# Weight loads of a recurrent attention loop: issued on a plan of TensorE's progress

## The chip, the cores and the metric

The kernel runs on one core of a Trainium2 chip. The metric is device microseconds per execution. All weights, the input and the output are bf16. Five engines work side by side and meet only through semaphores: TensorE (PE, with its weight loads as PEld), VectorE (DVE), ScalarE (ACT), GpSimd (POOL) and SyncE (SP). In this kernel SyncE issues nearly all DMA transfers of the loop, one after the other in the order of the program.

## What is computed

The input `x` has 2048 tokens of 640 numbers. Branch A is an attention layer with 32 heads of 192 that runs over 64 segments of 32 tokens. Each segment sees its own tokens and 8 memory tokens, and the layer's output for the memory tokens is the memory of the next segment, so the 64 segments follow one another. Branch B is a gated GELU layer. A sigmoid gate mixes the two.

```python
def _A_ref(x, mem0, Wq, Wk, Wv, Wo, seg_len):
    ...
    for s in range(n_seg):
        xs = x[:, s * seg_len:(s + 1) * seg_len, :].copy()
        h = jnp.concatenate([mem, xs], axis=1)
        q = jnp.einsum('btd,dhe->bhte', h, Wq)      # the same for k and v
        scores = jnp.einsum('bhqe,bhke->bhqk', q, k) * scale
        scores = jnp.where(mask[None, None], scores, -1000000000.0)
        p = _softmax(scores, axis=-1)
        o = jnp.einsum('bhqk,bhke->bhqe', p, v)
        o = jnp.einsum('bhte,hed->btd', o, Wo)
        mem = o[:, :M, :].copy()
        outs.append(o[:, M:, :])
...
g = _sigmoid((x * gate_w).sum(-1, keepdims=True))
return g * a + (1 - g) * b
```

## The kernel before, in words

A recording layer (`_Sched`) notes every operation with the regions of memory that it reads and writes, works out which operations must wait for which, and then writes one stream of instructions per engine, in the order in which the operations were noted. An engine that waits therefore holds up all that stands behind it in its stream.

Branch B and the gate run first. Then comes the loop: `segment(s)` walks through a list `PROG` of some hundred items, written out by hand, that says in which order the parts of a segment go to TensorE. The heads are cut into four octets. `("g", i, k)` is a step of the projections to Q, K and V (`proj`, row L1039, and L226 where the weights stay on TensorE); `sc` are the scores (L1080, L1088, L1093), `ex` the softmax, `pt` transposes the probabilities, `pv` multiplies them with V (L1172, L1174), `wo` is the output projection (L1201, and L1224 for the last octet). The items `lf`, `le`, `vb` and the rows L882, L887, L889, L893 are work for later segments, on eight tokens of each (the "left" tokens), which doesn't hang on the memory; they differ between segments, with a period of four, so segments fall into classes by s mod 4. `out_store`, `x_load`, `stg_load` (L932), `bz_load` and `left_store` (L893) are the other transfers of the loop, all on SyncE.

The weights take more room than the on-chip memory has. They are cut into pieces: 384 KB for one k step of Q, K or V of one octet, 480 KB for a pair of heads of Wo. Most pieces stay on the chip for good. 17 slots are shared by two pieces each: one of the octet that even segments use first and odd segments use last, and one of the octet at the other end. So in every segment the first octet's pieces in these slots are overwritten, once used, by the pieces that the last octet of the same segment needs: four of Q, five of K, five of V, three of Wo. The next segment walks through the octets the other way round, and finds what the last one loaded.

`swap_loads(seg, item)` is called after each item of `PROG`. It goes through the pieces used since the last call (`done_keys`) and notes a load (`load_piece`, L597) of the other piece of each shared slot at once. The load waits for the last matmuls that read the slot; nothing else holds it but its place in SyncE's stream. The K pieces of the first four projection steps are put behind the Q pieces (`later`).

Of the kernel before, what the change touches and what calls it, by code (L numbers as in the profile page):

```python
# [231 lines left out]
def _build(nc, A_x, A_mem0, A_Wq, A_Wk, A_Wv, A_Wo, seg_len, w_gate, w_up, w_down,  # L232
# [34 lines left out]
    S_ = _Sched(nc)  # L267
# [84 lines left out]
    def bview(o, nbytes, plo=0, phi=128):  # L352
        return arena[plo:phi, o // 2:(o + nbytes) // 2]
# [4 lines left out]
    def sreg(o, nbytes, plo=0, phi=128):  # L358
        return Rg("sb", o, o + nbytes, plo, phi)
# [129 lines left out]
    def piece_src(key):  # L489
        if key[0] == 3:  # L490
            return Wo2[:, key[1]]
        m, o_, k = key
        return (Wq2, Wk2, Wv2)[m][:, k, OW * o_:OW * (o_ + 1)]

    def piece_size(key):
        return GO if key[0] == 3 else GQ

    def piece_view(key, o):
        if key[0] == 3:
            return bview(o, GO).rearrange("p (c n) -> p c n", n=Dm)  # L500
        return bview(o, GQ)
# [59 lines left out]
    res_off = {}  # L561
# [8 lines left out]
    r_res = {key: sreg(o, piece_size(key)) for key, o in res_off.items()}  # L570
# [21 lines left out]

    loaded = {}

    def load_piece(key, name):
        loaded[slot_id[key]] = key
        S_.add("sp", lambda e: e.dma_start(piece_view(key, res_off[key]), piece_src(key)), writes=[r_res[key]],  # L597
               dma_sem="slot%d" % slot_id[key], name="%s %s" % (name, key))

    def piece(seg, key):  # L600
        order = orders[seg % 2]
        oi = last_req.get(seg, -1) + 1
        assert order[oi] == key, "pieces must be consumed in order"
        last_req[seg] = oi
        if seg == 0 and key in tmp_off:
            return left_piece(key)
        done_keys.append(key)
        return piece_view(key, res_off[key]), r_res[key]

    def swap_loads(seg, item):  # L610
        if item[0] == "g" and item[1] == 0 and 0 < item[2] < KT - 1:
            later.extend(key for key in done_keys if key[0] == 1)
            done_keys[:] = [key for key in done_keys if key[0] != 1]
        elif later:
            done_keys[:] = sorted(done_keys + later, key=lambda key: key[:1] + key[2:])
            del later[:]
        for key in done_keys:
            other = swap_in.get(key)
            if other is None or (other in partner) == (seg % 2 == 0):
                continue  # L620
            load_piece(other, "swap s%d" % seg)
        del done_keys[:]

    def left_piece(key):
        if key in tmp_off:
            return piece_view(key, tmp_off[key]), r_tmp[key]
        return piece_view(key, res_off[key]), r_res[key]
# [6 lines left out]
    def load_residents(cls, pick=lambda key: True):  # L634
        for key in first:
            if slot_class[key] == cls and pick(key):
                load_piece(partner[key] if key in tmp_off else key, "res")
# [39 lines left out]
    for h in range(NH):  # L677
        for w_, sb_, rw_, nm in ((w_gate, wg_sb, r_wg, "wg"), (w_up, wu_sb, r_wu, "wu")):
            S_.add("sp", lambda e, h=h, w_=w_, sb_=sb_: e.dma_start(
                sb_[h], w_.rearrange("(p k) f -> p k f", p=128)[:, :, FH * h:FH * (h + 1)]),  # L680
                writes=[rw_[h]], dma_sem="%s%d" % (nm, h))
# [228 lines left out]
    for n, (g, o) in enumerate(units):  # L910
# [7 lines left out]
        if g == 0:  # L918
            S_.add("pool", lambda e, o=o, b=b: e.tensor_copy(out=stg[:, o], in_=lst[b][:, 0]), reads=[r_lst[b]], writes=[r_stg[o]],
                   name="stg s0 o%d" % o)  # L920
# [344 lines left out]
    def segment(s):  # L1265
# [3 lines left out]
        for n, item in enumerate(PROG):  # L1269
# [48 lines left out]
            else:  # L1318
# [3 lines left out]
                if q == 3 and item != items[-1]:  # L1322
                    wo_left(s, held)
            swap_loads(s, item)
            if s == 0 and item == ("g", 0, KT - 1):
                load_residents(3, lambda key: key[0] < 3 and on_tmp(key))
# [63 lines left out]
def bass_gated_mix__memory_aug_recurrent_mem_tr__glu_gated_geglu__prompt_kernel(  # L1390
    nc,
    A_x,
    A_mem0,
    A_Wq,
    A_Wk,
    A_Wv,
    A_Wo,
    A_seg_len,
    B_x,
    B_w_gate,  # L1400
    B_w_up,
    B_w_down,
    gate_w,
    out,
):
    _build(nc, A_x, A_mem0, A_Wq, A_Wk, A_Wv, A_Wo, A_seg_len, B_w_gate, B_w_up, B_w_down, gate_w, out)
# [33 lines left out]
```

## Time and profile before

| | |
|---|---|
| median of three runs | 1797.18 us (1792.85 to 1797.43) |
| span of the profiled execution, first to last instruction | 1783.4 us |
| median less that span | 13.8 us |
| granted TensorE clock, mean | 0.998 |
| HBM read over the span | 498.00 MB |
| transfers issued at L597: K, V, Q, Wo | 335, 335, 272, 205 |
| L597 from issue to landing, least / median / most | 3.0 / 7.7 / 15.7 us |

The page tells the profiled execution's span but not its time by the clock that the runs are timed with. What lies around the span is therefore taken as the difference to the median, 13.8 us (9.5 us to the fastest run). In the profile, a line such as `PE ps L1224 <- DMA arena<-in_A_Wo_dram: 12.6, 22, 0.9` says that TensorE's instructions of line 1224 stood idle for 12.6 us in all, 22 times and 0.9 us at the longest, until a transfer from Wo had landed. In a timeline a line shows the start, the length, engine, line and operation, how many were merged, and in brackets the idle time before it with what ended it.

### The profile page before, as it was taken

What the parts mean: (1) busy time and instruction counts of PE and PEld (TensorE: products, weight loads), DVE (VectorE), ACT (ScalarE), POOL (GpSimd) and SP (SyncE); (2) the same over time, 40 slices, a digit from 0 to 9 for tenths busy, and PEclk for the clock granted to TensorE, in tenths of its full rate; (3) what the DMA queues carried; (4) which work ended last, traced back from release to release, by engine and by line L of the source; (5) the groups of instructions that cost most, each with busy time, mean ns of one, the idle gap of its engine ahead of it and who ended that gap; (6) DMA issues with size and microseconds to landing.
All of it is one profiled execution on the core that took longest, in us unless ns stands there. A gap on an engine that the chain in (4) does not pass through costs nothing.

```text
span 1783.4 us, 80070 instructions
## 1 busy us (share of the span) xinstructions
PE 1629.5 (91%) x39162; PEld 817.9 (46%) x31501; DVE 957.7 (54%) x2932; ACT 793.8 (45%) x1835; POOL 319.8 (18%) x1099
## 2 busy tenths in 40 slices
PE   9999989899998999899899999899999989899987
PEld 4554444454444444454444444454444444454443
DVE  2223555555555655555565655555555655555554
ACT  3222444444444444444444444444444544444443
POOL 1100111111211111111111111111211111111211
PEclk9999999999999999999999999999999999999999
DMA  9815887888788887888788887888888887888786
GB/s 332 297 45 177 329 318 266 324 322 316 289 295 298 318 311 261 318 318 315 287 299 299 311 319 263 322 310 319 298 299 300 317 290 269 321 313 321 289 303 260
DMA packets 263390, 524.33 MB, mean 294 GB/s; under 512 B 97384, under 2 KB 116224, under 8 KB 263040
## 3 DMA queue, kind: packets, MB, share of 16 engines
q1 hardware_dynamic: 259912, 516.11, 79.5%
q8 instruction: 276, 4.52, 1.0%
q10 hardware_dynamic: 3128, 3.09, 0.5%
q14 instruction: 74, 0.61, 0.1%
HBM read 498.00 MB, written 21.11 MB: 291 GB/s over the span
## 4 chain that ended last, share of the span: by engine, by line
PE 69%; DMA 13%; DVE 8%; ACT 6%; issue 4%; SPq 0%; DVEq 0%; ACTq 0%
PE ps L1039 20%; PE ps L226 15%; PE ps L1201 8%; DMA arena<-in_A_Wv_dram 7%; PE ps L1172 3%; DMA left_qk_scratch<-arena 3%; PE ps L802 3%; PE ps L799 3%; PE ps L882 3%; DVE arena L889 3%; PE ps L1093 2%; PE ps L817 2%; ACT arena L887 2%; PE ps L1080 2%; PE ps L1088 2%
## 5 line engine op out<-in xcount | busy, mean ns | idle before, releaser
L1039 PE MATMUL ps<-arena 128*32 128x384 bf16 x9940 | 734.8, 328 | 58.5 <-DVE arena L1344 40.4
L226 PE MATMUL ps<-arena 128*32 128x384 bf16 x7680 | 584.4, 326 | 10.8 <-ACT arena L887 6.1
L1039 PEld LDWEIGHTS ps<-arena 128*32 128x32 bf16 x9940 | 254.0, 96 | 420.1 <-issue 244.4
L1073 DVE STREAM_TRANSPOSE arena<-arena 128x384 bf16<-128x384 bf16 x512 | 279.0, 564 | 227.0 <-ACT arena L1059 226.6
L1059 ACT ACTIVATE arena<-ps 128x384 bf16<-128x384 f32 x512 | 236.2, 489 | 176.3 <-PE ps L1039 164.4
L1201 PE MATMUL ps<-arena 128*32 128x320 bf16 x6144 | 297.0, 300 | 16.1 <-issue 15.5
L1201 PEld LDWEIGHTS ps<-arena 128*32 128x32 bf16 x6144 | 163.6, 97 | 75.7 <-issue 26.5
L1119 ACT ACTIVATE ps<-ps 104x160 f32<-104x160 f32 x256 | 74.3, 290 | 236.4 <-DVE ps L1109 236.4
L1107 DVE TENSOR_REDUCE arena<-ps 104x4 f32<-104x160 f32 x256 | 83.1, 325 | 176.0 <-PE ps L1093 175.7
L1157 ACT ACTIVATE arena<-ps 128x448 bf16<-128x448 f32 x192 | 104.8, 546 | 143.3 <-PE ps L1144 143.3
L1191 POOL COPY arena<-arena 128x96 bf16<-128x96 bf16 x256 | 68.4, 267 | 522.6 <-ACT arena L1183 419.3
L936 POOL COPY arena<-arena 128x96 bf16<-128x96 bf16 x256 | 70.0, 274 | 498.7 <-PE ps L1093 436.3
L1183 ACT ACTIVATE arena<-ps 128x480 bf16<-128x480 f32 (+1 forms) x256 | 138.1, 540 | 34.0 <-PE ps L1174 29.0
L1062 ACT ACTIVATE arena<-ps 128x384 bf16<-128x384 f32 x256 | 124.8, 488 | 52.7 <-PE ps L1039 52.4
L1172 PE MATMUL ps<-arena 128*64 128x160 bf16 x1536 | 122.1, 243 | 10.4 <-issue 3.4
L1172 PEld LDWEIGHTS ps<-arena 128*64 128x64 bf16 x1536 | 80.6, 109 | 97.9 <-ACT arena L1157 46.6
L882 PE MATMUL ps<-arena 128*32 128x384 bf16 x1280 | 111.1, 330 | 1.2 <-issue 1.2
L1174 PE MATMUL ps<-arena 128*64 128x64 bf16 x1536 | 105.1, 194 | 5.8 <-issue 5.8
L1121 DVE TENSOR_REDUCE arena<-ps 104x4 f32<-104x160 f32 x256 | 81.8, 320 | 51.6 <-ACT ps L1119 43.9
L889 DVE STREAM_TRANSPOSE arena<-arena 128x384 bf16<-128x384 bf16 x128 | 73.8, 577 | 57.4 <-ACT arena L887 52.6
L1224 PE MATMUL ps<-arena 128*32 128x160 bf16 x3072 | 77.1, 234 | 22.2 <-DMA arena<-in_A_Wo_dram 12.6
L887 ACT ACTIVATE arena<-ps 128x384 bf16<-128x384 f32 x128 | 62.4, 490 | 67.6 <-DVE arena L889 38.5
(84 smaller groups left out, 1816.7 us busy)
## 6 DMA issues: line engine op xcount, KB each, us to landing
arena<-in_A_Wk_dram SPq DMA_DIRECT2D x335, 384.0 KB, 7.7
arena<-in_A_Wv_dram SPq DMA_DIRECT2D x335, 384.0 KB, 9.4
arena<-in_A_Wq_dram SPq DMA_DIRECT2D x272, 384.0 KB, 5.6
arena<-in_A_Wo_dram SPq DMA_DIRECT2D x205, 480.0 KB, 7.4
left_qk_scratch<-arena SPq DMA_DIRECT2D x64, 192.0 KB, 2.6
arena<-left_qk_scratch SPq DMA_DIRECT2D x63, 192.0 KB, 7.8
ffn_b_scratch<-arena ACTq DMA_DIRECT2D x16, 160.0 KB, 3.7
arena<-ffn_b_scratch SPq DMA_DIRECT2D x64, 40.0 KB
```

The lines of the kernel that those rows point to most:

```text
L226: return e.add_instruction(mybir.InstMatmult(name=nm, start_tensor_calc=like["start"], stop_tensor_calc=stop, tile_size=(128, 32), tile_po ...
L882: fns.append(lambda e, outp=outp, rhs=rhs, j=j: e.matmul(outp, lhs, rhs, start=(k == 0), stop=(k == KT - 1), tile_position=(0, 32 * j)))
L889: S_.add("dve", lambda e: e.transpose(out=dst[:, :, m].rearrange("p q c i -> p c q i"), in_=rowl.rearrange("p (c r) -> p c r", r=L)), read ...
L1039: fns.append(lambda e, outp=outp, rhs=rhs, j=j: e.matmul(outp, lhs, rhs, start=(k == 0), stop=(k == KT - 1), tile_position=(0, 32 * j)))
L1059: S_.add("act", lambda e, m=m, bk=bk: e.activation(out=rows_sb[m], in_=ps[:, bk, 0:384], func=ACTF.Copy), reads=[r_ps[bk]], writes=[r_rows ...
L1062: S_.add("act", lambda e, i=i, bk=bk: e.activation(out=v_sb[i % NVB].rearrange("p (c n) -> p c n", c=3), in_=ps[:, bk, 0:384].rearrange("p ...
L1073: S_.add("dve", lambda e: e.transpose(out=dst[:, :, 0:L], in_=rows_sb[m].rearrange("p (c r) -> p c r", r=L)), reads=[r_rows[m]], writes=[r ...
L1157: S_.add("act", lambda e: e.activation(out=PT, in_=ps[:, bank, 0:PTW + 128], func=ACTF.Copy), reads=[r_ps[bank]], writes=[r_PT], name="pT ...
L1172: return [lambda e: e.matmul(full, v[:, e0:e0 + 64], PTm[:, i], start=True, stop=False, tile_position=(0, 64 * i), skip_group_check=True), ...
L1174: lambda e: e.matmul(part, vl[:, e0:e0 + 64], PTl[:, i], start=False, stop=True, tile_position=(0, 64 * i), skip_group_check=True)]
L1183: S_.add("act", lambda e: e.activation(out=apx(u[:, 0, 0, :], [[R, na], [3 * R, 4], [1, R]]), in_=ps[:, A, 0:na * W].rearrange("p (c t r) ...
L1201: fns.append(lambda e, i=i, t=t, j=j, gv=gv: e.matmul(ps[32 * j:32 * j + 32, bank, 0:2 * DJ].rearrange("p (h n) -> p h n", h=2), lhs2[i], ...
```

## The change

Loads are no longer noted in the moment in which a slot comes free. `swap_loads` puts the piece into a list `queued`. A counter, `clock[0]`, adds up a planned duration for each matmul that has been put into TensorE's stream so far, by the table `STEP` (in ns, by kind of work). After each item of `PROG`, as long as that counter has reached the next due time `clock[2]`, one piece is taken from the list and its load is noted; the due time then moves on by `PACE`, 1080 ns, or to the counter, if that is further. The load gets one more dependency: it waits for the operation that was then the last in TensorE's stream. At the last item of `PROG` the list is emptied. The loads keep their order among themselves, but other transfers of SyncE's stream now stand elsewhere between them: the output store and the x load before the K loads instead of among the V loads, the load of L932 before the Wo loads or before the last of them instead of behind them.

```diff
-    def load_piece(key, name):
+    def load_piece(key, name, after=None):
         loaded[slot_id[key]] = key
-        S_.add("sp", lambda e: e.dma_start(piece_view(key, res_off[key]), piece_src(key)), writes=[r_res[key]],
+        op = S_.add("sp", lambda e: e.dma_start(piece_view(key, res_off[key]), piece_src(key)), writes=[r_res[key]],
                dma_sem="slot%d" % slot_id[key], name="%s %s" % (name, key))
+        if after is not None:
+            op.deps.add(after)
...
     def swap_loads(seg, item):
...
             if other is None or (other in partner) == (seg % 2 == 0):
                 continue
-            load_piece(other, "swap s%d" % seg)
+            queued.append(other)
         del done_keys[:]
+        clock[0] += sum(STEP.get(op.name.split()[0], 0) * len(op.fns) for op in S_.streams["pe"][clock[1]:])
+        clock[1] = len(S_.streams["pe"])
+        while queued and (clock[0] >= clock[2] or item == PROG[-1]):
+            load_piece(queued.pop(0), "swap s%d" % seg, S_.streams["pe"][-1])
+            clock[2] = max(clock[0], clock[2] + PACE)
+
+    PACE = 1080
+    STEP = dict(Q=41, K=41, V=41, Vl=41, LQ=41, LK=41, mask=60, sc=30, pT=15, pTl=15, PV=45, PVa=45, Wo=26, Wol=34)
+    queued = []
+    clock = [0, 0, 0]
```

In a segment of class 2 (s mod 4 = 2) the seventeen loads are tied to these operations, in this order: K of octet step 0, k = 0, 1 and 4; K of octet step 1, k = 1; the scores of step 0; K of step 1, k = 4; Q of step 2, k = 3; the scores of step 1; P-V of step 0; Q of step 3, k = 1; the scores of step 2; P-V of step 1; K of step 3, k = 3; P-V of step 2 (the last V load); the scores of step 3; V of step 3, k = 2; V of step 3, k = 4 (the last Wo load). In classes 0 and 1 the last Wo load is tied to the scores of step 3, in class 3 to V of step 3, k = 1.

## The prediction

> **What bounds the kernel now.** I read the page first, then one segment of the loop: TensorE's waits, the busy time by stretches, SyncE's issues, the landing times of single transfers, TensorE's timeline. The page:
>
> ```profile
> PE 1629.5 (91%) x39162; PEld 817.9 (46%) x31501; DVE 957.7 (54%) x2932; ACT 793.8 (45%) x1835; POOL 319.8 (18%) x1099
> q1 hardware_dynamic: 259912, 516.11, 79.5%
> ```
>
> TensorE is 91% busy, SyncE's queue has the 16 DMA engines at 79.5%. Neither number says which limits, so segment 30 (929 to 953 us) in stretches (PE, PEld, DVE, ACT, POOL, clock, DMA share, GB/s):
>
> ```profile
> 928.00:932.00 4.00, 3.08 (x89) 0.94 (x37) 2.17 (x8) 0.93 (x3) 1.14 (x4) 1.00 0.40 94
> 932.00:936.00 4.00, 4.00 (x110) 1.54 (x62) 2.98 (x10) 1.78 (x5) 0.53 (x2) 1.00 1.00 373
> ...
> 948.00:952.00 4.00, 3.45 (x100) 1.75 (x80) 1.98 (x6) 2.61 (x6) 1.18 (x4) 1.00 0.64 231
> ```
>
> For some 18 us the DMA engines are full at about 400 GB/s; TensorE loses time at the end, where that burst runs out. The segment's issues on SyncE (start, length, transfer, count):
>
> ```profile
> 929.75 0.58 SPq L597 DMA_DIRECT2D arena<-in_A_Wk_dram  x1
> 930.37 1.85 SPq L597 DMA_DIRECT2D arena<-in_A_Wq_dram  x4
> 932.27 1.90 SPq L597 DMA_DIRECT2D arena<-in_A_Wk_dram  x4
> 934.21 2.46 SPq L597 DMA_DIRECT2D arena<-in_A_Wv_dram  x4
> 937.90 1.11 SPq L597 DMA_DIRECT2D arena<-in_A_Wv_dram  x1
> 941.65 1.28 SPq L597 DMA_DIRECT2D arena<-in_A_Wo_dram  x3
> 942.98 0.43 SPq L932 DMA_DIRECT2D arena<-left_qk_scratch  x1
> ```
>
> Issued in 13 us, served in 22. Three windows of the DMA view, each around one issue (last column: us to landing) - the first load, the last V load, the last Wo load:
>
> ```profile
> arena<-in_A_Wk_dram SPq DMA_DIRECT2D x1, 384.0 KB, 3.6
> ...
> arena<-in_A_Wv_dram SPq DMA_DIRECT2D x1, 384.0 KB, 9.9
> ...
> arena<-in_A_Wo_dram SPq DMA_DIRECT2D x1, 480.0 KB, 9.0
> ```
>
> So the first lands at 933.3, the last V at 937.9+9.9 = 947.8, the last Wo at 942.5+9.0 = 951.5: a chain of about 1 us per load. TensorE meets it here:
>
> ```profile
> 943.93 0.20 PE L1174 MATMUL ps<-arena 128*64 128x64 bf16 x2
> 946.76 0.35 PE L1039 MATMUL ps<-arena 128*32 128x384 bf16 x4 [0.57 <-DMA arena<-in_A_Wv_dram]
> 947.87 0.35 PE L1039 MATMUL ps<-arena 128*32 128x384 bf16 x4
> 950.27 0.81 PE L1224 MATMUL ps<-arena 128*32 128x160 bf16 x36
> 951.58 0.58 PE L1224 MATMUL ps<-arena 128*32 128x160 bf16 x12 [0.50 <-DMA arena<-in_A_Wo_dram]
> ```
>
> Two waits, 1.07 us in this segment. Over the whole run, in TensorE's waits:
>
> ```profile
> PE ps L1224 <- DMA arena<-in_A_Wo_dram: 12.6, 22, 0.9
> PE ps L1039 <- DMA arena<-in_A_Wv_dram: 9.3, 19, 1.6
> PE ps L1039 <- DMA arena<-in_A_Wk_dram: 3.5, 11, 0.6
> ```
>
> 25.4 us in all: the most that better landing times could return.
>
> **The change, part by part.** No transfer, byte or matmul is added or removed; some of TensorE's matmuls signal more, which I cost at nothing (no row shows a price for a signal; a segment has over a hundred already). What moves is when each of the 17 loads of a segment is issued: one per 1.08 us of planned TensorE time, after the item last placed. The planned rates agree with the trace: 41 ns per projection matmul, and 946.93 to 947.34 is 12 Wo matmuls at 34 ns on the clock, planned 26. A segment's plan adds up to 22.1, 21.3, 19.6 and 22.1 us for s mod 4 = 0, 1, 2, 3; the 17th load goes out near 16 x 1.08 = 17.3 us. That leaves 4 us or more of planned work in three classes and 2.3 us in class 2, to which segment 30 belongs.
>
> *The seventeenth load, class 2.* It is tied to the last V group, the row at 947.87, which ends at 948.2. It can't be issued before 948.3; today that is 942.5. How long does it take? The least of the L597 loads took 3.0 us, the first of a segment 3.6 here (over segments 2 to 61 its median is 3.7, the second's 4.3). A Wo piece is 480 KB against 384, 0.24 us more at the chain's step of 0.98. Taking 3.6+0.24, it lands at 952.2; at 3.0+0.24, at 951.6; at 4.3+0.24 with the 192 KB load of L932, now queued before the Wo loads (about 0.5 us), at 953.3. Today 951.5, and TensorE arrives at 951.1. Extra wait 0.7 us, bounds 0.1 and 1.8; I take 0.7, as few loads are then queued, like the first of a segment. 16 segments: +11 us (+1 to +29).
>
> *The last V load, class 2.* Tied to the P-V group of octet step 2 (rows 943.93), so issued at 944.2; at 3.6 it lands at 947.8, today 947.8, needed at 947.87. 0, upper bound 0.7 x 16 = +11.
>
> *The V load before it.* Tied to the K group that ends at 942.0, it could land at 945.7 instead of 946.7 and end the 0.57 us wait. But the twelve loads before it need the engines: 933.3 + 12 x 1.0 to 1.1 = 945.3 to 946.5. Gain between 0 and 0.57; the same wait stands in class 1 (0.56 at 1024.39). Over 32 segments 0 to -18 us; I take -6, nearer to nothing, because the chain's steps average above 1.05 in the trace (some steps are 1.6 to 1.8).
>
> *Class 1.* The trace's segment 33 waits 0.93 us for its last Wo (landed 1029.6, wanted 1028.8). Its new step ends at 1022.9, so it is never too late; the queue decides, and in that queue the 192 KB load now stands ahead of it: 0 to +0.5 us, 16 segments, +6 taken (0 to +8), or less than nothing if the queue has caught up (down to -15).
>
> *Classes 0 and 3.* New steps for the last Wo end at 996.8 (segment 32) and 971.7 (segment 31), wanted at 1003.4 and 977.7: 6 us for a load that takes 4. Covered by the projections and Wo in between; nothing, unless the load takes over 6 us.
>
> *What else is moved in SyncE's queue.* The out store and the x load now stand before the Wk loads. The store waits for VectorE's last mix; in segment 30 that is done at 929.9, three us before its turn: nothing. The left_qk store waits for VectorE and stands ahead of Wo loads in class 1; it already does today for the last of them. A load that waits for its step holds up what is queued behind it: the 192 KB load and the b load. The first lands at about 948.5 instead of 952 and is wanted in the next segment: no cost.
>
> The Trainium skill speaks against the change too (DMA: Bandwidth & Descriptors, Rules for kernel authors): issue a DMA early, compute, wait for it late, so that its fixed cost is covered. The trace agrees for the seventeenth load of class 2, whose cover shrinks from 8.6 to 2.9 us; by that rule no term of the sum would be below zero.
>
> Sum: +11 + 0 - 6 + 6 = +11 us. The span goes from 1783.4 to about 1794; the median lies 13.8 above the span, so 1797.2 + 11 = **1808**.
>
> **The rivals.**
> *Faster: the queue catches up.* If spaced loads take nearer to 3.0 us and the engines keep up, the V waits of classes 1 and 2 go (-18) and the last Wo of class 2 is late by only 0.25 (+4): 1783. For it: the V loads spend up to 10 us between issue and landing today, most of it queued. Against: the queue is full because the bytes take that long. It decides if landings after 941 are gate plus 3.2 or less. The Trainium skill (the same page, Latency and other measured facts) states that the HBM part of a DMA's fixed cost grows under load and is smaller when lighter. No run here yet shows a load amid spaced traffic. Chance 0.25.
> *The same: it changes nothing that counts.* The spacing, 1.08, is close to the chain's own step, 1.0 to 1.1. If all landings stay set by the queue, only issue times move: 1797. Against: the seventeenth load of class 2 can't land as early as today. Chance 0.2.
> *Much slower: a spaced load still takes 4.3 us or more, and a wait delays the next step and so the next issue.* Last Wo +1.4, last V +0.7 in class 2, the 0.5 of class 1: 16 x 2.6 = +42: 1839; with half of the class 2 terms, 1822. Chance 0.12.
>
> **How the numbers follow.** Forecast case 0.43, with the much slower rival 0.55 slower; 0.2 the same; 0.25 faster. About 0.3% (5.4 us) is what a measurement of this kernel can tell from no change. The range goes from a little under the faster rival, 1780, to past half of the much slower one, 1826. Slower cases alone: 1803 to 1830.
>
> **What would show it.** Right: TensorE's wait for in_A_Wo grows, in segments with s mod 4 = 2, to about 1.2 us; the L597 transfers' median landing falls from 7 to 9 us to 4 to 6; DMA share in the full stretches falls a little below 1.00; the V waits hardly fall. Wrong: waits for in_A_Wv gone and none longer for in_A_Wo (faster rival), landings after the 13th load unchanged to 0.2 us (same), or K and V waits in every class (much slower).

## The result, and the profile after

The changed kernel takes 1883.7 us (median of four runs, 1882.55 to 1883.99) against 1795.0 us for the kernel before beside it (1792.14 to 1797.43): a ratio of 1.048, 95% interval 1.045 to 1.051. It is 89 us slower; the prediction had said 11, and its range ended at 1826.

The runs give each execution's time beside its span: 1.7 to 1.9 us lie around it, in every run here. The 13.8 us that the prediction put there were mostly something else: the profiled execution of before was some 10 us faster than the median of these four runs. So the two spans, 1783.4 and 1881.9 us, differ by 98.5, the medians by 89.

The page of the kernel after, busy time of TensorE and share of SyncE's queue:

```profile
PE 1671.5 (89%) x39162; PEld 811.5 (43%) x31501; DVE 961.9 (51%) x2932; ACT 794.8 (42%) x1835; POOL 320.3 (17%) x1099
q1 hardware_dynamic: 259912, 516.11, 79.1%
```

The same 39162 instructions and the same bytes. The 98.5 us fall into two parts: TensorE is busy for 42.0 us more (1671.5 less 1629.5) with the same work, and idle for 56.5 us more. The idle part is in TensorE's waits (us in all, times, longest):

```profile
PE ps L1236 <- DMA arena<-in_A_Wo_dram: 80.1, 81, 2.9
PE ps L1051 <- DMA arena<-in_A_Wv_dram: 33.9, 61, 2.2
PE ps L1051 <- DMA arena<-in_A_Wk_dram: 16.0, 40, 1.1
```

L1236 and L1051 are the lines 1224 and 1039 of before. The three rows grew from 25.4 to 130.0 us; other waits shrank by about half as much, those for VectorE by 19 us and those put down to "issue" by 31 (below). The landing times that belong to them, from the page's DMA issues (KB each, median us from issue to landing), first before, then after:

```profile
arena<-in_A_Wv_dram SPq DMA_DIRECT2D x335, 384.0 KB, 9.4
...
arena<-in_A_Wo_dram SPq DMA_DIRECT2D x205, 480.0 KB, 7.4
```

```profile
arena<-in_A_Wv_dram SPq DMA_DIRECT2D x335, 384.0 KB, 5.7
...
arena<-in_A_Wo_dram SPq DMA_DIRECT2D x205, 480.0 KB, 5.9
```

A spaced load does land sooner after its issue, but not in 3.6 us. Over segments 4 to 61, the seventeenth load is issued 18.2 us after the first instead of 14.1, which is 4.1 later; its median latency falls from 8.0 to 6.3, which is 1.7. So it lands more than 2 us later, in the mean of all classes. In class 2, for which the prediction worked it out, it is issued 19.9 us after the first, takes 5.1 and lands 3.2 us later in the segment than before. The mean period of a segment (from its first projection matmuls to those of the next, segments 4 to 62) by s mod 4 = 0, 1, 2, 3 was 25.07, 25.56, 23.90, 25.35 us and is 25.54, 26.71, 27.11, 26.47: class 2 loses 3.2 us and the others 0.5, 1.2 and 1.1. (One long period, 31 us for segment 62, is 0.3 of the 3.2.)

Segment 30 (class 2) again, whose first load goes out at 973.8 here. SyncE's issues of it, merged by transfer:

```profile
977.53 0.58 SPq L963 DMA_DIRECT2D out_dram<-arena  x1
...
978.68 3.45 SPq L597 DMA_DIRECT2D arena<-in_A_Wk_dram  x4
982.56 6.06 SPq L597 DMA_DIRECT2D arena<-in_A_Wv_dram  x5
988.66 0.43 SPq L944 DMA_DIRECT2D arena<-left_qk_scratch  x1
989.41 3.92 SPq L597 DMA_DIRECT2D arena<-in_A_Wo_dram  x3
```

The last Wo load is issued at 993.0, 19.2 us after the first (the prediction had 948.3 less 929.75, 18.5), and takes 5.1 us; it lands at 998.1. Before it come a Wo load that took 5.7 and one that took 6.2. The busy time in stretches (PE, PEld, DVE, ACT, POOL, clock, DMA share, GB/s), two of after and then one of before, shows that the engines did not become free:

```profile
978.00:982.00 4.00, 4.00 (x114) 1.97 (x82) 3.02 (x10) 3.15 (x9) 0.53 (x2) 1.00 1.01 345
982.00:986.00 4.00, 3.78 (x102) 1.76 (x74) 2.68 (x9) 2.72 (x7) 1.07 (x4) 1.00 1.02 351
```

```profile
940.00:944.00 4.00, 3.58 (x96) 1.99 (x88) 1.91 (x7) 2.46 (x6) 0.61 (x3) 1.00 1.03 410
```

By their busy share the DMA engines are about as full as before, with some 350 GB/s where before they moved about 400. It is about the rate at which loads are issued: 384 KB per 1.14 us, the mean step between two issues, is 345 GB/s. With 5.5 us per load, still about five loads share the engines. TensorE meets the landings here:

```profile
990.66 0.35 PE L1051 MATMUL ps<-arena 128*32 128x384 bf16 x4 [0.28 <-DMA arena<-in_A_Wv_dram]
991.61 0.35 PE L1051 MATMUL ps<-arena 128*32 128x384 bf16 x4 [0.61 <-DMA arena<-in_A_Wv_dram]
...
996.82 0.39 PE L1236 MATMUL ps<-arena 128*32 128x160 bf16 x12 [0.80 <-DMA arena<-in_A_Wo_dram]
998.14 0.39 PE L1236 MATMUL ps<-arena 128*32 128x160 bf16 x12 [0.94 <-DMA arena<-in_A_Wo_dram]
999.17 0.51 PE L1051 MATMUL ps<-arena 128*32 128x384 bf16 x4 [0.64 <-DVE arena L1356]
```

These four waits make 2.63 us (one of 0.5 us for a K load stands earlier in the segment), where before had two of 1.07. And the last row is something else: four projection matmuls, which take 0.35 us in the first two rows, now take 0.51. The stretches around that place, cut at the edges of the granted clock:

```profile
991.79:995.20 3.41, 3.29 (x88) 1.60 (x68) 1.16 (x4) 2.08 (x5) 0.30 (x2) 1.00 0.94 321
995.20:998.62 3.42, 1.49 (x48) 0.68 (x48) 1.19 (x3) 0.59 (x2) 0.77 (x3) 1.00 0.62 208
998.62:1002.03 3.41, 2.86 (x37) 0.74 (x21) 1.16 (x5) 0.00 (x0) 1.01 (x4) 0.50 0.36 87
```

After a window of 3.4 us in which TensorE was busy for 1.49, the next 3.4 us run at a granted clock of 0.50: the end of this segment and the start of the next. The records of the clock hold 2 such half-clock stretches (8.7 us) in before and 22 (96.9 us) in after, each of one or two windows of 3.4 us, one of them in either kernel at its very end. Of the 96.9 us, 58 begin in segments of class 2, 24 in class 1, 10 in class 0. The expectations below call these stretches windows. TensorE was busy for 79.3 us of them (3.4 in before). At half clock the rows of four projection matmuls start 0.32 us apart instead of 0.16, so about half of those 79.3 us is added time: some 38 of the 42 us of longer busy time.

What the fall of the clock goes with can be read by cutting the whole trace of after into windows of this length, at these edges. Each of the 21 stretches inside the loop follows a window in which TensorE was busy for a share of 0.23 to 0.48. Of the windows at full clock that half clock did not follow, only two were as low (0.47); the next had 0.50. In before, one window of 0.54 was followed by half clock and one of 0.49 was not. So about half a window of work is where the clock falls here. The Trainium skill's page TensorE: Matmul & The Clock Gate (Part 1: The HAM clock gate) describes free-running windows of 3413 ns and a clock of either half or full. The trace agrees to the figure (windows of 3.413 us, 0.50 or 1.00). The rule that this page of the Trainium skill gives, in HAM oscillation — how this bites in real kernels, is to leave no idle gap on TensorE above some 3.4 us. Here no wait for weights was longer than 2.9 us, and in the window above none longer than 0.94, and the clock fell all the same. So the measurement decides against a single long gap as the condition.

### The profile page after: what moved, and what is told of

Its sections match the earlier page's. It is cut to its first block, busy times and chain, and to the rows that moved or that the text cites. A ratio compares the mean times of both kernels' runs of the same rounds, so it can differ in the third digit from the quotient of the medians.

```text
span 1881.9 us, 80055 instructions
## 1 busy us (share of the span) xinstructions
PE 1671.5 (89%) x39162; PEld 811.5 (43%) x31501; DVE 961.9 (51%) x2932; ACT 794.8 (42%) x1835; POOL 320.3 (17%) x1099
## 4 chain that ended last, share of the span: by engine, by line
PE 57%; DMA 34%; DVE 4%; ACT 3%; issue 1%; SPq 0%; POOLq 0%; POOL 0%; DVEq 0%; ACTq 0%
DMA arena<-in_A_Wo_dram 19%; PE ps L1051 18%; PE ps L226 14%; DMA arena<-in_A_Wk_dram 8%; DMA arena<-in_A_Wv_dram 6%; PE ps L1213 5%; PE ps L814 3%; PE ps L811 3%; PE ps L1184 2%; PE ps L1105 2%; PE ps L829 2%; PE ps L1092 2%; PE ps L1100 2%; PE ps L1236 2%; ACT arena L1169 1%
## 5 line engine op out<-in xcount | busy, mean ns | idle before, releaser
L1051 PE MATMUL ps<-arena 128*32 128x384 bf16 x9940 | 758.7, 337 | 83.1 <-DMA arena<-in_A_Wv_dram 33.9
L226 PE MATMUL ps<-arena 128*32 128x384 bf16 x7680 | 607.1, 338 | 9.9 <-ACT arena L899 4.1
L1051 PEld LDWEIGHTS ps<-arena 128*32 128x32 bf16 x9940 | 257.0, 98 | 495.5 <-issue 259.3
L1071 ACT ACTIVATE arena<-ps 128x384 bf16<-128x384 f32 x512 | 236.2, 489 | 260.9 <-PE ps L1051 243.3
L1213 PE MATMUL ps<-arena 128*32 128x320 bf16 x6144 | 282.6, 299 | 1.0 <-issue 1.0
L1213 PEld LDWEIGHTS ps<-arena 128*32 128x32 bf16 x6144 | 156.6, 96 | 51.5 <-DVE arena L1165 2.4
L1236 PE MATMUL ps<-arena 128*32 128x160 bf16 x3072 | 87.7, 237 | 88.4 <-DMA arena<-in_A_Wo_dram 80.1
L1074 ACT ACTIVATE arena<-ps 128x384 bf16<-128x384 f32 x256 | 124.9, 488 | 52.5 <-PE ps L1051 52.2
L1236 PEld LDWEIGHTS ps<-arena 128*32 128x32 bf16 x3072 | 53.8, 96 | 137.3 <-DMA arena<-in_A_Wo_dram 98.7
L894 PE MATMUL ps<-arena 128*32 128x384 bf16 x1280 | 107.9, 329 | 0.0
```

The costliest lines, as they stand in the source:

```text
L226: return e.add_instruction(mybir.InstMatmult(name=nm, start_tensor_calc=like["start"], stop_tensor_calc=stop, tile_size=(128, 32), tile_po ...
L894: fns.append(lambda e, outp=outp, rhs=rhs, j=j: e.matmul(outp, lhs, rhs, start=(k == 0), stop=(k == KT - 1), tile_position=(0, 32 * j)))
L1051: fns.append(lambda e, outp=outp, rhs=rhs, j=j: e.matmul(outp, lhs, rhs, start=(k == 0), stop=(k == KT - 1), tile_position=(0, 32 * j)))
L1071: S_.add("act", lambda e, m=m, bk=bk: e.activation(out=rows_sb[m], in_=ps[:, bk, 0:384], func=ACTF.Copy), reads=[r_ps[bk]], writes=[r_rows ...
L1074: S_.add("act", lambda e, i=i, bk=bk: e.activation(out=v_sb[i % NVB].rearrange("p (c n) -> p c n", c=3), in_=ps[:, bk, 0:384].rearrange("p ...
L1213: fns.append(lambda e, i=i, t=t, j=j, gv=gv: e.matmul(ps[32 * j:32 * j + 32, bank, 0:2 * DJ].rearrange("p (h n) -> p h n", h=2), lhs2[i], ...
```

## The experiments

The theory after this reading: at a spacing of 1080 ns of plan, the stock of queued loads is gone, a load still takes 5 to 6 us because the engines are shared, so the landings fall behind TensorE; its waits hold up the next tied issue, and they push the clock to half. The rivals: the moved order in SyncE's queue; lateness of the Wo loads alone; a smaller number of loads in flight, without any lateness; the clock as a mere consequence without a price.

### The order alone, the ties left out

```diff
-            load_piece(queued.pop(0), "swap s%d" % seg, S_.streams["pe"][-1])
+            load_piece(queued.pop(0), "swap s%d" % seg)
```

> The changed kernel with its order of SyncE's queue (out store and x load ahead of the K loads, the 192 KB load ahead of the Wo loads), but without the tie of each load to a TensorE step: a load waits only for its slot. Theory THIN (a spaced queue holds some five loads, and so few keep the DMA engines at about 340 instead of 400 GB/s): the queue is deep again, so within 0.5% of the kernel before, 1790 to 1806 us. Theory LATE (only the last loads of a segment come too late): the same. Theory ORDER (the small transfers moved ahead of the loads cost the time): most of the 89 us stays, 1860 us or more.

Measured: 1807.4 us, ratio 1.008 (1.005 to 1.010), just above what THIN and LATE expected and far from ORDER. The seventeenth load lands 18.97 us after the first one's landing instead of 18.21, and TensorE's wait for Wo grows to 26.9 us; there are 8 half-clock stretches. The moved order by itself costs about 0.8%, some 14 us. The prediction had costed it at nothing.

### Half the spacing

```diff
-    PACE = 1080
+    PACE = 540
```

> The changed kernel with PACE 540 instead of 1080: ties stay, but the last V load of class 2 is tied to the scores of octet step 1 and the Wo loads go out as their slots come free. Theory THIN: the loads are issued at twice the rate at which they are served, so the queue fills; DMA at 380 GB/s or more in the full stretches, 1795 to 1815 us. Theory LATE: nothing is late any more, 1797 plus or minus 5. Theory ORDER: out store and x load now stand behind nine loads, so about half comes back, 1840. If the tie itself costs (more signals, SyncE waiting), the time stays above 1830.

Measured: 1792.0 us, ratio 1.001 (0.999 to 1.004). Landing of the seventeenth 18.33, periods within 0.35 us of before: half the spacing is as good as no spacing, about as LATE had it, and the tie itself has no price that shows.

### Wo loads not spaced

```diff
-        while queued and (clock[0] >= clock[2] or item == PROG[-1]):
+        while queued and (clock[0] >= clock[2] or queued[0][0] == 3 or item == PROG[-1]):
```

> The changed kernel, but Wo loads are not paced (they follow as soon as the list reaches them); Q, K and V stay at 1080. In class 2 the three Wo loads are then tied to P-V of step 2 (at 14.5 us of the segment) instead of 15.6, 17.2 and 19.2. Theory LATE, as the prediction has it: the last Wo load was the loss, so at most 1820 us and no half-clock windows. Theory THIN: the V loads and the queue ahead of Wo are as thin as before, Wo gains 1 to 1.5 us in classes 2 and less in the others: 1840 to 1865 us, V and K waits unchanged (34 and 16 us in all).

Measured: 1836.0 us, ratio 1.023 (1.018 to 1.028), 16 half-clock stretches, between what LATE and THIN expected. TensorE's waits, with both rows far above those of before (9.3 and 12.6):

```profile
PE ps L1051 <- DMA arena<-in_A_Wv_dram: 39.6, 61, 2.6
PE ps L1236 <- DMA arena<-in_A_Wo_dram: 32.7, 43, 1.5
```

About half of the loss comes back. Late Wo loads are not the whole: the V loads, spaced as in after, keep their waits, and the seventeenth load still lands 19.75 us after the first, against 18.21 in before and 20.88 in after.

### Before, with at most five loads in flight

```diff
+        if name.startswith("swap"):
+            flight.append(op)
+            if len(flight) > DEPTH:
+                op.deps.add(flight[-1 - DEPTH])
+
+    DEPTH = 5
+    flight = []
```

> The kernel before, but each weight load of the loop also waits until the load five places earlier has landed, so that at most five are in flight; no tie to TensorE, nothing spaced by plan, and the engines always have four loads waiting. Theory THIN in its strict form (few loads in flight lower the throughput): loads land 5 us after issue at a step of 1.1 to 1.2 us, 1850 us or more. Theory GAPS (it is not the number in flight but that a spaced issue leaves the engines short whenever a load is late): steps stay near 1.0 to 1.05, 1797 to 1820 us.

Measured: 1827.0 us, ratio 1.017 (1.012 to 1.023), between the two theories. No plan and no tie to TensorE, yet from the sixth on loads take 5 to 7 us in the median, a packet of 3072 B takes 0.137 us (before 0.132, after 0.138) and one of 3840 B 0.164 (0.154, 0.169), and the seventeenth load lands at 19.50. Between the landings of the sixth and the thirteenth load, the engines move 352 GB/s with 4.8 loads in flight on average; after has 357 with 4.8, before 400 with 6.6, and the spacing of 800 below 404 with 6.6. So a short queue goes with slower packets, a lower rate and later landings here, without any plan that would set the rate. It also costs a wait on SyncE, which holds up other transfers: class 1 grew most, by 1.65 us, which is not the pattern of after. The run shows that few loads in flight have a price, not how much of the 89 us it is.

### Class 2 not spaced

```diff
-        while queued and (clock[0] >= clock[2] or item == PROG[-1]):
+        while queued and (clock[0] >= clock[2] or seg % 4 == 2 or item == PROG[-1]):
```

> The changed kernel, but in segments with s mod 4 = 2 every load goes out as soon as its slot is free; the other three classes stay paced at 1080. Class 2's period went from 23.90 to 27.11 us between the two kernels, the others by 0.5, 1.2 and 1.1. Theory PLACE (the loss is made in the segment that has the shortest plan, as the prediction had it): 16 x 3.2 = 51 us come back, 1825 to 1840 us, and class 2's period is 24.0 to 24.5. Rival SPREAD (a late segment only passes on what the paced ones before it owe; all classes lose alike once one does not): less than 30 us come back, 1850 us or more.

Measured: 1826.3 us, ratio 1.017 (1.012 to 1.023); class 2 takes 24.61 us instead of 27.11, class 3 25.64 instead of 26.47. By the medians, some 57 us of the loss come back when the quarter of the segments with the shortest plan is left unspaced, a good 10 of them in the class 3 segments that follow. The rest stays in classes 0 and 1, where the prediction had nothing and +6.

### The ties in the old order

```diff
-            load_piece(queued.pop(0), "swap s%d" % seg, S_.streams["pe"][-1])
+            queued.pop(0).deps.add(S_.streams["pe"][-1])
```

(The lines are in short, against after.) Here each load keeps its place in SyncE's stream as before and gets only the dependency.

> The kernel before with its own order of SyncE's queue, and only the tie: each load, noted where it was, also waits for the TensorE step that the plan of 1080 ns gives it. Out store, x load and the 192 KB load stay where they were, and so wait behind paced loads. Theory THIN+LATE (spacing is the cost, the order adds the 14 to 16 us that order_only showed): 1860 to 1872 us. Rival ORDER x SPACING (the small transfers hurt more in a thin queue): 1845 us or less.

Measured: 1868.8 us, ratio 1.045 (1.040 to 1.050), 18 half-clock stretches, as THIN+LATE expected. The spacing alone costs some 78 us; with the 14 to 16 of the order, the two add up to a little over the 89 measured.

### Work for TensorE in its waits

```diff
+                if item[2] or n_:
+                    ...
+                    S_.add("pe", [lambda e, fb=fb: e.matmul(...) for _ in range(2)], reads=[r_ident], writes=[r_ps[fb]], name="fill")
```

Two matmuls of 128x512 without use, ahead of each of the last three Wo pieces of a segment.

> The changed kernel with two extra 128x512 matmuls of a constant (into a free bank, never read; 0.43 us by 0.215 each) ahead of each of the last three Wo pieces of a segment, where TensorE waits. Nothing else moves. Theory CLOCK (the 22 windows at half clock, 97 us, are set off by those waits, and cost some of the 42 us by which TensorE's busy time grew): the half-clock windows fall below 6 and the time falls by 15 to 40 us, to 1844 to 1868. Rival (half clock costs nothing, because the transfers set the pace anyway): windows vanish and the time stays within 8 us of 1883, or rises by what of the 82 us of added matmuls is not covered.

Measured: 1890.3 us, ratio 1.056 (1.053 to 1.060), which is what the rival expected and not CLOCK. Half-clock stretches fall from 22 to 7. But a pair of the added matmuls takes 0.6 us, not 0.43, so 116 us of TensorE's time were added, and they show up in classes that had too little wait to hide them: class 0 goes from 25.54 to 26.71 us, while class 2 falls from 27.11 to 26.72. Price and gain can't be told apart in this run, so the filler was then confined to class 2:

```diff
-                if item[2] or n_:
+                if s % 4 == 2 and (item[2] or n_):
```

> The kernel after, with two added 128x512 matmuls, whose result nobody reads, ahead of each of the last three Wo pieces in segments with s mod 4 = 2 only; there TensorE waits for the load anyway. CLOCK (half-clock windows that follow the waits cost time by themselves): the windows that lie at the end of class 2 segments (58 us of 92 in the loop) go, the period of class 2 falls from 27.1 to 25.6 us, the other classes stay within 0.2, and the time falls by 16 to 28 us to 1855 to 1868. COVERED (transfers alone set the pace and the half clock hides in the waits): class 2 stays above 26.8 and the time within 5 us of 1884, or above.

Measured: 1863.0 us, ratio 1.041 (1.035 to 1.046). By the medians that is 21 us faster than after, by the ratios some 13, with more matmuls and no load moved in the program. The intervals of the two ratios touch, so the gain is clear only just. Half clock goes from 96.9 to 60.6 us, in stretches that begin in class 2 from 58.0 to 13.7. The wait for Wo falls too, for the most part because the filler itself (29 us of TensorE's time) now runs where TensorE waited:

```profile
PE ps L1242 <- DMA arena<-in_A_Wo_dram: 46.7, 54, 2.2
```

Class 2 falls less than expected, from 27.11 to 26.58, and class 3, which was expected to stay, from 26.47 to 25.47: a stretch that begins at the end of a class 2 segment slows the start of the next. So the half clock has a price of its own, 0.4 to 0.6 us for each of its us here (13 to 21 us for 36); for the 97 us of after that would be, as an estimate, 35 to 55 us of the 89. The 38 us of slower matmuls agree.

### Half the bytes, spaced and not spaced

```diff
+        cut = (lambda v: v[0:64]) if name[:4] == "swap" else (lambda v: v)
-        ... e.dma_start(piece_view(key, res_off[key]), piece_src(key)) ...
+        ... e.dma_start(cut(piece_view(key, res_off[key])), cut(piece_src(key))) ...
```

The same edit in after and in before: the loop's loads move 64 of 128 partitions.

> The kernel after, but each load of the loop's swaps moves only partitions 0 to 63 of its piece (half the bytes, the same packets of 3072 and 3840 B), so half of each swapped slot keeps the other octet's weights: this kernel's time tells about the transfers, not about a valid output. Issue times by plan are unchanged. SHARE (a spaced load took 5.5 us because some five loads share the engines): with half the bytes a load takes at most 3.5 us at every position, the waits of TensorE for Wo, Wv and Wk fall from 130 to under 20 us, half-clock windows to 3 or fewer, and the time to 1765 to 1800. FIXED (5.5 us is what a load issued alongside others takes, whatever its bytes): latencies stay at 4.5 us or more, waits over 70 us, time above 1840.

> The kernel before with the same halved loads of the loop: the floor for half_spaced. Its 25 us of waits for weights should go to under 5, so 1765 to 1780 under both theories. SHARE expects half_spaced within 0.5% of this one; FIXED expects half_spaced over 3% slower than this one. If this kernel stays at 1790 or above, the waits for weights were no part of the time of before.

Measured: 1771.4 us (ratio 0.989, 0.985 to 0.994) spaced and 1771.3 us (0.989, 0.985 to 0.993) not spaced. With half the bytes the spacing costs nothing, and the theory of a latency that bytes don't change is out. But the other one is not right to the letter either: median latencies by place run from 3.2 to 4.6 us, not up to 3.5, the waits for weights are 34 us, not under 20, and of 12 half-clock stretches, where 3 were expected, 10 are in class 2. Nor were the engines relieved by half: a packet now takes 0.199 us (spaced) and 0.227 us (not spaced) where after has 0.138, so a halved load still takes 72% (spaced; 86% not spaced, against the 0.132 of before) of a whole one's engine time. Two rows each of TensorE's waits, spaced first, then not spaced:

```profile
PE ps L1237 <- DMA arena<-in_A_Wo_dram: 31.8, 51, 3.6
...
PE ps L1214 <- issue: 4.1, 3, 2.0
```

```profile
PE ps L1202 <- issue: 11.0, 15, 2.2
...
PE ps L1225 <- DMA arena<-in_A_Wo_dram: 0.7, 1, 0.7
```

The same total by different waits: the spaced kernel pays 31.8 us for Wo and saves nearly as much in "issue", which over all lines is 4.1 us against 35.0. The same fall is there between before and after, from 36.5 to 5.4 us. In before, nearly all of these stalls (36.2 us) end 2.2 to 2.6 us after the last 16 KB packet of an instruction queue has started. So the spaced kernels save some 30 us in this kind of wait, which after loses again in others. That the loads' burst is what holds such a packet up is a guess that fits, not shown by itself.

### A spacing of 800

```diff
-    PACE = 1080
+    PACE = 800
```

> The kernel after with PACE = 800 ns for 1080. The engines' own step in before was 1.0 to 1.1 us per load. STOCK (the loss comes once the spacing takes away the stock of queued loads, so it sets in at the engines' own step): 800 still builds a stock, the seventeenth load lands within 0.6 us of before's 18.2 us after the first, waits under 45 us, time 1795 to 1815 (order_only's order would alone give 1807). GRADUAL (each ns of spacing costs alike, from 540 with 1792 to 1080 with 1884): 1832 to 1842, last landing at 19.4 or later.

Measured: 1789.3 us, ratio 0.999 (0.997 to 1.001), as STOCK had it but for a time even lower than it expected. The seventeenth load is issued at 14.4 us and lands 18.24 after the first, as in before, and the waits are nearly those of before:

```profile
PE ps L1236 <- DMA arena<-in_A_Wo_dram: 13.2, 26, 1.0
...
PE ps L1051 <- DMA arena<-in_A_Wv_dram: 11.0, 24, 0.6
```

The loss doesn't grow with the spacing from 540 on; it sets in between 800 and 1080. The real time between two issues is longer than planned, since a segment planned at 19.6 to 22.1 us takes 24 to 26: 800 becomes some 0.9 us of real time, 1080 becomes 1.14 in the mean of after. The engines' own step between landings in before is 1.04 us from the sixth load to the thirteenth. The reading is that below it the queue sets the landings and above it the plan does; no run lies between 0.9 and 1.14 to show where it turns. The cost of the order isn't seen here either: in class 2 the load of L944 stands behind the Wo loads again, and the store of L963 behind one K load.

### A store out of the way

Before, and the left_qk store at the end of a segment (L893) is held back until the first projection step group of the next one has been noted, so that the first loads of that segment go out ahead of it.

```diff
-        if m:
+        if m and hold:
+            held_stores.append(unit(s, u))
+        elif m:
...
+            if item == ("g", 0, KT - 1):
+                while held_stores:
+                    left_store(*held_stores.pop(), 3)
...
-            left_evac(s, *i)
+            left_evac(s, *i, hold=True)
```

> The kernel before with one move: the left_qk store that is noted at the end of a segment goes into SyncE's queue after the first group of projection steps of the next segment, so the loads of that segment don't stand behind it. In class 1 they do today (first load issued 1.0 us after its slot was free, 16 segments). Theory CHAIN (the loop runs at the pace of the chain of loads, first issue to last landing): class 1's period falls from 25.6 by 0.7 to 1.0, 11 to 16 us in all, 1778 to 1786 us. Rival (TensorE's own work sets the pace): within 5 us of before.

Measured: 1785.7 us, ratio 0.997 (0.995 to 0.999), the only kernel with whole loads whose interval lies below both before and after. The waits for Wo and Wv fall to

```profile
PE ps L1039 <- DMA arena<-in_A_Wv_dram: 5.9, 13, 0.7
...
PE ps L1224 <- DMA arena<-in_A_Wo_dram: 4.9, 11, 1.0
```

from 9.3 and 12.6, mostly in class 1, whose first load now goes out 1.0 us sooner. Yet class 1's period stays at 25.53 us, so CHAIN's sign did not come: other waits took the place of those for weights. The two profiled executions are about equally long (1784.2 and 1783.4 us), so they don't show where the 5 us of the medians lie. What can be said is that issuing weights sooner shortened the waits for them and cost nothing.

## Why the prediction was wrong

The direction was right, the size off by a factor of eight. By its own steps:

- **The seventeenth load, class 2 (+11, up to +29).** This is the step that failed, and most of the others hang on it. The latency of 3.6+0.24 us was taken from a load that finds the engines empty, and 4.3 was the bound; the median in class 2 is 5.1 (over all classes the last four loads take 5.6, 5.6, 5.8 and 6.3). The issue comes later too, in class 2 19.9 us after the first load instead of 18.5, because waits for V and K hold up the step to which it is tied. Together the load lands 3.2 us later than before, where 0.7 was forecast. TensorE's wait for Wo in class 2 grew from 0.3 to 2.0 us a segment: the upper bound of +29, not +11. "Few loads are then queued" was true of SyncE's side and false of the engines': in segment 30 the two Wo loads before it, which landed at 995.6 and 996.8, were still in flight when it went out at 993.0.
- **The last V load (0) and the V load before it (-6).** The same latency: in class 2 the last V load takes 4.2 us instead of 3.6 and lands 1.5 later in the segment than before, and V waits over the run rose from 9.3 to 33.9 us instead of falling.
- **Classes 0 and 3 (nothing, "6 us for a load that takes 4") and class 1 (+6).** The seventeenth load takes 6.5 us there, the cover is gone, and the condition that the text itself set, "unless the load takes over 6 us", was met: TensorE waits for Wo 13 and 9 us in classes 0 and 3, where before had no such wait, and 21 instead of 8 in class 1. Periods rose by 0.5, 1.1 and 1.2 us. Of 16 segments each, that is some 44 us that the sum had nearly at zero. Class 3's part is hardly its own loads': with the half clock of class 2 mostly gone its period is 25.47 us, against 25.35 in before.
- **The planned time taken for time.** The text left 2.3 us of planned work in class 2 behind a seventeenth load at 17.3 planned us, and called 1.08 close to the chain's own step. Plan and trace differ by 13 to 22%, and the experiments at 540, 800 and 1080 fit a turn at that step.
- **What else is moved in SyncE's queue (nothing).** The order by itself costs some 14 us.
- **The clock, missing from the sum.** The prediction took the granted clock as it was. 42.0 us of the span's growth are longer busy time of TensorE with the same work, some 38 of them at half clock; the filler in class 2 showed that they aren't wholly hidden in the waits.
- **The gain that it didn't see.** "Issue" stalls fell by 31 us and waits for VectorE by 19. The rows of before (36.5 us of "issue" over all lines) could have raised the question.
- **The rivals.** The much slower one named the mechanism, a load of 4.3 us or more and waits that delay the next issue, with its sign of waits for K and V in every class (all but K in class 0). Its price was too low, 1822 to 1839, for the reasons above: 4.3 was not the latency, and neither the classes 0 and 3 nor the clock were in it. The "catches up" rival needed landings 3.2 us after the gate; the least among the last four loads took 3.8. The Trainium skill's rule that the prediction cited (DMA: Bandwidth & Descriptors, Rules for kernel authors), to issue early and wait late, pointed the right way. In these runs later issue of whole loads never won time, and the one run that issued them sooner won 0.3%.
- **What would show it.** Median landings fell to 4.7 to 5.9 us, as the text said, and the DMA share in the burst (sixth to thirteenth landing) fell from 1.04 to 0.99. But the wait for Wo in class 2 is 2.0 us, not 1.2, and the V waits rose. Part of the sign for its own forecast was thus there, and so was that of the much slower rival.

What stays open: why engines at nearly the same share move some 350 instead of 400 GB/s when about five loads are in flight, how much of the 89 us that is, and how the 57 us of idle and the 42 us of longer busy time feed each other through the ties.

## What to carry to other kernels

A load's latency alone on the engines is no estimate for a load amid a stream: if the stream already fills the engines, later issue means later landing, and by these runs spacing is free only as long as its real step stays under the engines' own (here 1.04 us; 800 planned ns, 0.9 in real time, were free, and 1080, 1.14 in real time, cost 5%). Work out a pacing table in measured time, not in planned time, and give every class of the loop its own check of the cover. When waits are added near a point where TensorE is already half idle over some 3.4 us, look at the granted clock, and count its slow windows as a term of the sum.

## What had not been expected of the hardware

- A granted clock of 0.50 for windows of 3.413 us after a window with TensorE busy for less than about half of it (0.23 to 0.48 in the loop of after), with no single wait for weights above 2.9 us.
- Packets of 3072 B take 4 to 5% longer and packets of 3840 B 6 to 10% longer with about five loads in flight (after, and five at most) than in before, with 6.6, and the rate in the burst is 352 to 357 GB/s instead of 400, at a DMA share of 0.99 to 1.00 instead of 1.04. Loads of 64 partitions take 72 to 86% of the engine time of 128.
- TensorE's "issue" stalls, 36.5 us in before, fall to 4 to 13 us in the runs with a short queue of loads in all segments, and nearly all of them in before end 2.2 to 2.6 us after a 16 KB packet of an instruction queue has started.
